# The first group of output weights, loaded as 112 partitions at once and the other 16 two by two

## The chip, the core and the metric

The kernel runs on one core of one Trainium2 chip. The metric is the device time in microseconds (us) of one execution; several executions are timed and their median is given. A profile of one further execution shows what each engine and the DMA queues did in it. TensorE is called PE there, VectorE DVE, ScalarE ACT, GpSimd POOL and SyncE SP.

## The reference

One decode step of attention over a long cache, gated by a small network, with two batch rows, 32 query heads on 8 key heads, 32768 cached keys and a head size of 128, all in float32:

```python
xn = _layernorm(x, axis=-1)                                  # x: 2 x 1 x 512
q = (xn @ wq)                                                # 32 heads of 128
scores = jnp.einsum("bhqd,bhkd->bhqk", q, k) * (Dh ** -0.5)  # k, v: 2 x 8 x 32768 x 128
p = _softmax(scores, axis=-1)
o = jnp.einsum("bhqk,bhkd->bhqd", p, v)
s = o.reshape(B, Sq, Hq * Dh) @ wo                           # wo: 4096 x 512
g = _silu(_B_ref(xn, w1, b1, w2, b2))                        # relu squared network, 512-1792-512
return x + s * g
```

The two caches are 537 MB of the 561 MB that are read. Each value of them is used for the four query heads of its key head and then never again.

## The kernel before, in words

There are 16 sequences (`s`), one for each pair of a key head and a batch row. Keys and values of a sequence come in two halves each, 8 MB a half, 128 partitions of 64 KB. Keys go to `kslots` (three slots of 32 KB a partition, of which a half takes two), values to `vbuf` (64 KB a partition). For a quarter of a sequence's keys `scores` (L240) turns them with DVE transposes (L249) and multiplies them with the query on PE (L254); `softmax` and `probs` make the weights; `values` (L307) multiplies them with the value half (L315).

All the large loads are issued by SP, in the order of the list `loads` (L137 to L142). Each entry names an event and is issued as soon as the event has been given (`give`, L155). The end of the list reads:

```python
    loads += [(("s", NK - 2), load_v, NV - 2), (("v", NV - 3), load_v, NV - 1)]
    loads += [(("s", NK - 1), load_wo, 0), (("s", NK - 1), load_wo, 1), (("v", NV - 2), load_wo, 2), (("v", NV - 2), load_wo, 3)]
```

So the next to last value half goes to `kslots`, the last one to `vbuf`, and behind them come the four groups of output weights, `load_wo(0)` to `load_wo(3)` (L121 to L131). A group is 1024 rows of `wo`, 2 MB, laid out as 128 partitions of 16 KB; two groups share one slot of `kslots`. The first three are one load each (L127), the last is cut along the row into four pieces (`PIECES`, L130). In this document they are called group 0 to group 3, and the last two value halves V30 and V31.

SP takes its instructions in order, and each load carries the waits that the scheduling framework gave it: for what was written or read in its destination before, and one more. The framework gives every load one of eight completion semaphores in turn (they are called semaphore 0 to 7 here); a load that gets a semaphore whose last load SP doesn't know to have landed waits for that load first. In the program as built V30 has semaphore 2, V31 semaphore 3, group 0 semaphore 4, group 1 semaphore 5, group 2 semaphore 6 and the four pieces of group 3 semaphores 7, 0, 1 and 2. The final store on SP (L409) waits for semaphore 4.

At the end `project` (L394) multiplies the attention output with the four groups on PE (L397), group by group and then piece by piece, into one accumulator; two DVE instructions (L406, L407) apply the gate and the residual, and two small stores (L409) write the result.

Of the kernel before, what the change touches and what calls it, by code (L numbers as in the profile page):

```python
# [14 lines left out]
P = 128  # L15
# [15 lines left out]
NT = 4  # L31
HALF = 64 * 128
NEG = -3.0e38
PIECES = ((0, 4), (4, 6), (6, 7), (7, 8))


@with_exitstack
def gqa_decode_kernel(ctx: ExitStack, tc: tile.TileContext, x, kc, vc, wq, wo, w1, b1, w2, b2, out):
    nc = tc.nc
# [12 lines left out]
    NWG = HQ // WG  # L52
# [68 lines left out]
    def load_wo(i):  # L121
        if i % 2 == 0:
            wide[i // 2] = kslots[:, 2 - i].rearrange("p (i j e) -> p i j e", i=2, j=WG)
        t = wide[i // 2][:, i % 2]
        src = wo[i * WG * P:(i + 1) * WG * P, :].rearrange("(p j) e -> p j e", p=P)
        if i < NWG - 1:
            nc.sync.dma_start(t, src)  # L127
        else:
            for j0, j1 in PIECES:
                nc.sync.dma_start(t[:, j0:j1, :], src[:, j0:j1, :])  # L130
        return t  # L131
# [7 lines left out]
    for m in range(2, NV):  # L139
        loads += [(("s", 2 * m - 2), load_k, m), (("v", m - 3) if m > 2 else ("w", 1), load_v, m - 2)]  # L140
    loads += [(("s", NK - 2), load_v, NV - 2), (("v", NV - 3), load_v, NV - 1)]
    loads += [(("s", NK - 1), load_wo, 0), (("s", NK - 1), load_wo, 1), (("v", NV - 2), load_wo, 2), (("v", NV - 2), load_wo, 3)]  # L142
    past = {None}
    done = [0]
# [83 lines left out]
    for t in sc:  # L228
        nc.vector.memset(t, NEG)

# [141 lines left out]
    for n in range(NK):  # L372
        s, i = divmod(n, NT)
# [16 lines left out]

    a_ps = sc[0]
    wot = [take(load_wo, i) for i in range(NWG)]

    def project(i, j0, j1):  # L394
        for j in range(j0, j1):
            for g in range(NG):
                nc.tensor.matmul(a_ps[32 * g:32 * g + 32, :DE], oW[:, i, j, :], wot[i][:, j, g * DE:(g + 1) * DE],  # L397
                                 start=(i == 0 and j == 0), stop=(i == NWG - 1 and j == WG - 1))

    for i in range(NWG - 1):  # L400
        project(i, 0, WG)
    for j0, j1 in PIECES:
        project(NWG - 1, j0, j1)
# [29 lines left out]
```

## Time and profile before

| what | value |
|---|---|
| median of 3 runs | 1311.9 us (1311.33 to 1311.93) |
| the profiled execution | 1312.29 us, of which the span from first to last instruction is 1310.2 us |
| PE busy | 912.5 us, 70% |
| DVE busy | 669.9 us, 51% |
| ACT busy, POOL busy | 130.3 us, 14.9 us |
| read from memory | 561.01 MB, 428 GB/s over the span |
| chain that ended last | DMA 72%, DVE 21%, "issue" 4%, PE 3% |
| mean granted TensorE clock | 0.852 |

Busy time is the sum of what an engine was seen to work. The chain is followed back from the last instruction: at each step to what released it. "Issue" is time in which nothing that the profile shows was waited for. The line of tenths for DMA is the mean over 16 DMA engines, which matters here: it says 9 when all sixteen are busy, and also when one of them is not. The trace holds every single DMA packet with its start, length and size, and for every load the sixteen increments of its completion semaphore, so that the sixteen engines can be told apart: a packet of 64 KB takes about 2.42 us and the next of the same engine starts as it ends.

### The profile page before, as it was taken

To read this page: it belongs to the slowest core of one execution; us is meant where nothing else is said; L and a number is where in the kernel's file an instruction comes from. 1 tells how busy PE (TensorE), PEld (TensorE's weight loads), DVE (VectorE), ACT (ScalarE), POOL (GpSimd) and SP (SyncE) were. 2 spreads that over 40 slices of the span, in tenths; PEclk is the share of its full clock that TensorE was granted. 3 is DMA by queue.
4 is the path that set the end of the run, shared out by engine and by line. 5 is a ranking of instruction groups with operands and counts; after the bars stand their busy time and mean duration, and the time that the engine had idled before them with its cause. 6 is when DMAs were issued, how large, how long until landed. Compare 5 with 4: busy or idle time off the path is not lost.

```text
span 1310.2 us, 11827 instructions
## 1 busy us (share of the span) xinstructions
PE 912.5 (70%) x5054; PEld 230.9 (18%) x5054; DVE 669.9 (51%) x778; ACT 130.3 (10%) x429; POOL 14.9 (1%) x76
## 2 busy tenths in 40 slices
PE   3777675758857677775758767576885767777575
PEld 1221121212202121120212112121220212111023
DVE  2866654446655445665445565444665544566410
ACT  0020010201002020110202001020110202001020
POOL 0000000000000000000000000000000000000000
PEclk9988877888878898887889878778987879888888
DMA  9999999999999999999999999999999999999997
GB/s 404 432 441 435 429 439 426 435 430 433 433 432 433 437 431 433 429 437 429 435 435 427 439 424 439 428 437 437 427 437 428 433 435 431 435 429 431 427 435 307
DMA packets 11042, 561.76 MB, mean 429 GB/s; under 512 B 1239, under 2 KB 1259, under 8 KB 1646
## 3 DMA queue, kind: packets, MB, share of 16 engines
q1 hardware_dynamic: 10952, 561.00, 99.2%
q8 instruction: 39, 0.64, 0.2%
q14 instruction: 13, 0.11, 0.0%
q10 hardware_dynamic: 38, 0.02, 0.0%
HBM read 561.01 MB, written 0.00 MB: 428 GB/s over the span
## 4 chain that ended last, share of the span: by engine, by line
DMA 72%; DVE 21%; issue 4%; PE 3%; ACT 0%; SPq 0%; DVEq 0%
DMA kslots<-in_A_k_cache 66%; DVE kt L249 20%; DMA kslots<-in_A_wo 2%; DMA kslots<-in_A_v_cache 2%; DMA vbuf<-in_A_wq 2%; PE sc L212 1%; PE sc L254 1%; PE o_ps L315 0%; PE y_ps L364 0%; PE h_ps L346 0%; ACT p L275 0%; DVE qr L219 0%; ACT pT L293 0%; PE pT_ps L289 0%; PE sc L397 0%
## 5 line engine op out<-in xcount | busy, mean ns | idle before, releaser
L254 PE MATMUL sc<-kt,qz 128*16 128x512 f32 x2048 | 574.4, 670 | 304.8 <-DVE kt L249 282.9
L249 DVE STREAM_TRANSPOSE kt<-kslots 128x1024 f32<-128x1024 f32 x512 | 583.8, 1206 | 300.5 <-DMA kslots<-in_A_k_cache 300.5
L315 PE MATMUL o_ps<-vbuf,pT 128*16 128x512 f32 x1984 | 232.3, 597 | 10.9 <-DMA vbuf<-in_A_v_cache 10.9
L254 PEld LDWEIGHTS sc<-kt,qz 128*16 128x16 f32 x2048 | 91.4, 98 | 772.8 <-DVE kt L249 619.0
L275 ACT ACTIVATE p<-sc,nm 128x512 f32<-128x512 f32 x64 | 45.7, 740 | 964.9 <-DVE nm L271 964.9
L315 PEld LDWEIGHTS o_ps<-vbuf,pT 128*16 128x16 f32 x1984 | 59.1, 97 | 160.8 <-issue 146.0
L258 DVE TENSOR_REDUCE rm<-sc 128x1 f32<-128x512 f32 x64 | 43.1, 673 | 66.3 <-PE sc L254 66.3
L293 ACT COPY pT<-pT_ps 64x128 f32<-64x128 f32 x256 | 66.4, 259 | 22.6 <-PE pT_ps L289 18.0
L289 PE MATMUL pT_ps<-ident,p 128*128 128x128 f32 x256 | 49.8, 342 | 18.1 <-ACT pT L293 13.8
L327 DVE COPY oT<-oT_ps 128x4 f32<-128x4 f32 x16 | 2.6, 162 | 97.9 <-PE oT_ps L326 97.9
L299 DVE RECIPROCAL r<-l_ps 128x4 f32<-128x4 f32 x16 | 2.9, 182 | 75.5 <-PE l_ps L297 75.5
L289 PEld LDWEIGHTS pT_ps<-ident,p 128*128 128x128 f32 x256 | 36.4, 177 | 28.0 <-ACT pT L293 23.5
L278 DVE TENSOR_REDUCE l<-l 128x1 f32<-128x4 f32 x16 | 2.5, 157 | 49.4 <-ACT p L275 49.4
L235 POOL COPY qz<-qT 32x16 f32<-32x16 f32 x64 | 12.7, 198 | 1078.2 <-PE sc L254 1043.0
L326 PE MATMUL oT_ps<-rs,o_sb 128*128 128x4 f32 x128 | 16.9, 255 | 11.5 <-ACT o_sb L322 11.4
L326 PEld LDWEIGHTS oT_ps<-rs,o_sb 128*128 128x128 f32 x128 | 15.5, 191 | 25.6 <-ACT o_sb L322 25.6
L322 ACT COPY o_sb<-o_ps 128x512 f32<-128x512 f32 x16 | 9.4, 585 | 76.9 <-PE o_ps L315 76.9
L264 PE MATMUL mx_ps<-ident,rm 128*128 128x128 f32 x16 | 5.2, 323 | 14.6 <-DVE rm L262 14.6
L203 PE MATMUL xnT_ps<-ident,xn 128*128 128x128 f32 x4 | 1.1, 431 | 20.1 <-DVE xn L199 20.1
L275 ACT ACTIVATION_READ_ACCUMULATOR p<-sc,nm 128x1 f32 x64 | 12.2, 191 | 0.0
L297 PE MATMUL l_ps<-lh,ones 128*128 128x4 f32 x32 | 8.4, 333 | 3.1 <-ACT pT L293 2.6
L212 PE MATMUL sc<-vbuf,first 128*32 128x512 f32 x64 | 9.4, 751 | 1.6 <-DMA vbuf<-in_A_wq 1.6
(69 smaller groups left out, 119.3 us busy)
## 6 DMA issues: line engine op xcount, KB each, us to landing
kslots<-in_A_k_cache SPq DMA_DIRECT2D x4, 4096.0 KB, 19.4
vbuf<-in_B_w SPq DMA_DIRECT2D x2, 3584.0 KB
kslots<-in_A_wo SPq DMA_DIRECT2D x3, 2048.0 KB
kslots<-in_A_wo SPq DMA_DIRECT2D x1, 1024.0 KB
kslots<-in_A_wo SPq DMA_DIRECT2D x1, 512.0 KB
kslots<-in_A_wo SPq DMA_DIRECT2D x2, 256.0 KB, 31.9
vbuf<-in_A_v_cache SPq DMA_DIRECT2D x31, 30.5
kslots<-in_A_k_cache SPq DMA_DIRECT2D x30
```

What stands on the lines that cost most here:

```text
L212: nc.tensor.matmul(sc[f][32 * g:32 * g + 32, :], xnT[:, d, 0:32], wqt[:, d, cc * 512:(cc + 1) * 512], start=(d == 0), stop=(d == ND - 1))
L235: nc.gpsimd.tensor_copy(qz[s % 2][32 * a:32 * a + 32, :, a * REP:(a + 1) * REP], qT[32 * a:32 * a + 32, b, hkv].rearrange("p h e -> p e h"))
L249: nc.vector.transpose(r.rearrange("p e o w -> p o e w"), kt[:, g * NO:(g + 1) * NO, e0 * 32:(e0 + 2) * 32].rearrange("p o (e w) -> p o e w ...
L254: nc.tensor.matmul(sc[t][32 * g:32 * g + 4 * REP, :], qz[s % 2][:, e0 + e, :], kts[g][:, e].rearrange("p o w -> p (o w)"), start=(e0 + e = ...
L258: nc.vector.tensor_reduce(rm[s][:, t:t + 1], sc[t], axis=AX.X, op=ALU.max)
L275: nc.scalar.activation(p[:, :, t % 2, :, t // 2], sc[t].rearrange("p (o w) -> p o w", w=32), AF.Exp, bias=nm, scale=SCALE, accum_out=l4[:, ...
L289: nc.tensor.transpose(t_ps[:, j * P:(j + 1) * P], p[:, 4 * i + j].rearrange("p c w u -> p (c w u)"), ident)
L293: nc.scalar.copy(sb[64 * a:64 * a + 64, :, c, :, 4 * i:4 * i + 4, :].rearrange("p k g o h -> p o g k h"), v[:, :, :, :4 * REP].rearrange(" ...
L297: nc.tensor.matmul(t_ps[:, :REP], ones, lh, start=True, stop=True)
L315: nc.tensor.matmul(o[32 * g:32 * g + 16, :], pT[s][:, k, c, g, 4 * i:4 * i + 4, :].rearrange("p o h -> p (o h)"), vt[:, lo:lo + 4, :].rear ...
L322: nc.scalar.copy(o_sb, o)
L326: nc.tensor.matmul(t_ps[:, :REP], o_sb[:, i * DH:(i + 1) * DH], r4[:, i, :], start=(i == 0), stop=(i == 3))
```

## The change

Group 0 is loaded by nine instructions in place of one. The first takes partitions 0 to 111, and eight more take two partitions each, 112 and 113, 114 and 115, and so on to 126 and 127. The bytes are the same, and so are the destination, the place in the list and everything else.

```diff
+MAIN = 112
 PIECES = ((0, 4), (4, 6), (6, 7), (7, 8))
...
         t = wide[i // 2][:, i % 2]
         src = wo[i * WG * P:(i + 1) * WG * P, :].rearrange("(p j) e -> p j e", p=P)
-        if i < NWG - 1:
+        if i == 0:
+            nc.sync.dma_start(t[:MAIN], src[:MAIN])
+            for p in range(MAIN, P, 2):
+                nc.sync.dma_start(t[p:p + 2], src[p:p + 2])
+        elif i < NWG - 1:
             nc.sync.dma_start(t, src)
         else:
             for j0, j1 in PIECES:
                 nc.sync.dma_start(t[:, j0:j1, :], src[:, j0:j1, :])
```

The instructions of PE, DVE, ACT and POOL keep their number and order in the program as built. On SP the stretch after V31 reads, with the semaphore that each load uses and the waits that it carries:

```
load of 112 partitions        semaphore 4   waits: DVE
pairs 1 to 5                  5, 6, 7, 0, 1 waits: none
pair 6                        semaphore 2   waits: semaphore 2 (V30)
pair 7                        semaphore 3   waits: semaphore 3 (V31)
pair 8                        semaphore 4   waits: semaphore 4 (the load of 112)
group 1                       semaphore 5   waits: semaphore 5 (pair 1), DVE
group 2                       semaphore 6   waits: semaphore 6 (pair 2), PE
group 3, four pieces          7, 0, 1, 2    waits: the same semaphores (pairs 3 to 6), PE
store                                       waits: semaphore 4 (pair 8), DVE
```

## The prediction

> **What bounds the kernel now.** I began with the page's slices of DMA and the memory rate: all 40 slices but the last are full. Then the chain of waits, read at its end:
>
> ```profile
> 1228.25 0.03 issue
> ...
> 1237.50 29.45 DMA kslots<-in_A_v_cache
> 1266.95 0.04 issue
> 1266.99 5.15 PE o_ps L315 x32
> 1272.15 0.26 SPq L127
> 1272.41 0.04 issue
> 1272.45 0.44 SPq L130
> 1272.89 0.04 issue
> 1272.93 31.77 DMA kslots<-in_A_wo
> 1304.70 0.04 issue
> 1304.74 1.26 PE sc L397 x24
> 1306.01 0.02 issue
> 1306.02 0.47 PE sc L397 x8
> ```
>
> Columns are start, length and what. The kernel ends 0.5 us of PE, two DVE instructions and a store after the last piece of output weights has landed, and that load was issued 31.8 us before: the transfers are what takes time. Next I split the tail into windows (length; busy us and count of PE, PEld, DVE, ACT, POOL; granted clock; DMA share; GB/s):
>
> ```profile
> 1293.00:1297.00 4.00, 3.88 (x50) 1.93 (x42) 0.00 (x0) 0.58 (x1) 0.00 (x0) 1.00 1.03 429
> 1297.00:1299.00 2.00, 2.00 (x55) 1.76 (x58) 0.45 (x2) 0.17 (x1) 0.00 (x0) 1.00 0.95 391
> 1299.00:1301.00 2.00, 1.87 (x71) 1.60 (x60) 0.00 (x0) 0.00 (x0) 0.00 (x0) 1.00 0.63 262
> 1301.00:1303.00 2.00, 1.94 (x64) 1.69 (x64) 0.00 (x0) 0.00 (x0) 0.00 (x0) 1.00 0.55 227
> 1303.00:1305.00 2.00, 1.35 (x45) 1.10 (x47) 0.00 (x0) 0.00 (x0) 0.00 (x0) 1.00 0.45 170
> ```
>
> From 1299 on only some nine of sixteen DMA engines still work. The sixteen increments of V31's semaphore say the same: seven at 1279.55 to 1280.80, nine at 1283.88 to 1286.33. Linking the packets into sixteen chains (a packet starts where the last of its engine ended) shows why: 39 reads of 16 KB, the rows of the "instruction" queue, fall in turn on eight of the chains, five each, about 1 us a time, and a ninth chain lags without them. The late nine set the end; the early seven have 5 to 6.5 us to spare.
>
> Last I read SP's own waits (total us, times, longest), for what an SP instruction waits for besides its data:
>
> ```profile
> SPq L409 <- DMA kslots<-in_A_wo: 16.8, 1, 16.8
> SPq L409 <- DVE fin L407: 15.9, 1, 15.9
> ```
>
> The store needs nothing of the weights' load. It held SP from 1274.4 until group 0 had landed (sixteenth increment at 1291.22) because it shares semaphore 4 with group 0. So such a wait is real in the trace. Today it costs nothing, because nothing is queued behind it.
>
> **The change part by part.**
>
> *One row fewer on each late engine: a gain of 0.61.* Group 0 is 128 rows of 16 KB, eight an engine. A 16 KB packet follows the last after 0.61 us (eight rows: V31's last increment 1286.33, group 0's 1291.22, 4.89 us). With 112 rows each engine has seven: 4.28 us, so that load lands at 1290.61. No load of 112 rows is in the trace; if they spread unevenly, some engine keeps eight and the gain is nothing.
>
> *Sixteen rows on two engines: no cost.* The two-row loads in the trace (x and its four quarters, 2048 and 512 bytes a row) put one row on each of two chains, always the same two, and both of these are free of instruction reads and end among the early seven. I expect the eight pairs there: eight rows more, 4.9 us, against a lead of 5 to 6 us. The price if that cover is gone is a rival below. [...]
>
> *Nine issues in place of one: hidden until V31 lands.* L127's issues take 0.33 to 0.43 us each, some 3 us for eight more, from 1258 on, while the queue holds V30 and V31 (28 us of work). Pair 6 waits for V30, landed at 1266.95: hidden too.
>
> *Pairs 7 and 8: a stop of the queue.* Pair 7 waits for V31 (1286.33), pair 8 for the load of 112 (1290.61). Behind them on SP stand groups 1, 2 and 3, which today are issued by 1274.4. So when the load of 112 ends, no engine but the two of the pairs has a packet left; the early ones have been idle since 1284. Neither DVE nor PE holds group 1 at that point: the keys' slot is free since 1247 and pair 1 landed long before. From the landing at 1290.61:
> - SP wakes, 0.04 (the chain's "issue" pieces); pair 8 is issued: from 0.26 (ACT's two-row load of x, L73) to 0.66 (SP's four-row store, L409). I take 0.4, near SP's other issues (0.33 to 0.49).
> - Group 1's issue to first packet: from 1.02 (first load, issued 0.73, first packet 1.75; the sixteenth engine's at 2.37, so 1.64) to 1.53 (store, 1307.15 to 1308.68). I take 1.3.
> - A first packet from rest: at the start the first packets of 64 KB took 3.10 us to the next, later ones 2.42; 0.69. It could be nothing if the latency does not show for smaller packets.
> - 24 rows and the semaphore writes: from group 0's landing to the last piece's, 1291.22 to 1305.98, 14.76.
> - Packet's end to its increment: 0.47 (1305.53 to 1305.98; 1290.73 to 1291.22). It was inside the landing I start from, and is paid a second time.
> - The two instruction reads of the tail (1295.77 and 1303.05, as PE goes through the projection) took 1.0 and 1.55 us from two of the late chains, which had as much to spare against the last. After the stop all engines restart level, and one such read shows in full: 0 to 1.55, I take 1.0.
>
> Sum: 1290.61 + 0.04 + 0.4 + 1.3 + 0.69 + 14.76 + 0.47 + 1.0 = 1309.27, against 1305.98: **3.3 us later**. Low ends (0.3, 1.02, 0, 0) give 1307.2, +1.2; high ends (0.70, 1.64, 0.69, 1.55) give 1310.4, +4.4. PE's tail behind the last piece (0.47), the two DVE instructions and the store are as before. PE reaches group 0's product at 1295.2 today, after the last value product; pair 8's row lands at about 1293.5, before that, so PE does not become late.
>
> The profiled execution is 1312.29; with 3.3 it is 1315.6. It stands 0.4 above the median of 1311.9, so I predict **1315.2** for the median, 1313.1 to 1316.3 by the terms' own ends. About 0.2% (2.6 us, so 1314.5) is what a measurement of this kernel can tell from no change.
>
> **The rivals.**
>
> *A. The queue does not stop, and the balance is all that is seen* (the other side). If SP's waits end early enough that groups 1 to 3 are queued before the late engines run dry, those lose one row and the two early ones take the rest in their lead: 1305.98 - 0.61, that is **1311.3**. For it: the seven early chains' lead, and that the bytes do not change. Against it: the wait of L409, which lasted to group 0's landing, and pair 8 has the same semaphore. It decides at group 1's issue: before about 1289 (first packet 1.3 later, at the late engines' end) this case holds, after it mine.
>
> *B. The rows get in each other's way.* [...] With seven rows an engine, and with two engines on neighbouring partitions, two may have to share a path. At half speed each a pair takes 1.22; from the early chains' end of V31 (1280.3) with seven rows (4.3) and eight pairs (9.8) the two engines reach 1294.4, and 24 rows (14.7) bring them to 1309.1, still level with the others in my sum. What then counts is the load of 112: each row of a late engine that is shared adds 0.61, and with one to four such rows the time is 1315.8 to 1317.6, **1316.7** in the middle. For it: no row shows such a load, against it: none either. [...]
>
> *C. The pairs fall on late engines.* Then seven and eight rows behind V31 end at 1286.33 + 4.28 + 4.9 = 1295.5, and 24 more at 1310.3: +4.3, **1316.2**, and up to 9 late if they share a path as well (4.9 more). For it: chains that nearly coincide can be exchanged in my linking. Against it: the x loads' chains get no instruction read.
>
> **How the numbers follow.** Mine 0.60, A 0.17, B 0.17, C 0.05, anything else 0.01. Of mine about a fifth lies below 1314.5. So slower is 0.48 + 0.17 + 0.05 = 0.70, the same 0.12 + 0.17 = 0.29, faster 0.01. The range takes my own ends and most of B, 1313.0 to 1317.7; it leaves out A and C's far end.
>
> **What the profile of the changed kernel would show.** SP's waits should list the pairs' line waiting for V31 and then, some 4.3 us, for the load of 112, and group 1 issued at about 1291, not 1258. The tail in windows should show the DMA share near 0.1 for about 2 us around 1291.5, and afterwards close to 1 until nearly the end, since all engines restart level. V31 should land at 1286.3 as before. The load of 112 landing later than 1291 would be B; the last increments of the pieces on two engines alone, well behind the other fourteen, would be C; no gap, A. I would be wrong if the queue holds packets throughout, or if restarting it costs much less than 2.4 us.

## The result and the profile after

The changed kernel takes 1323.7 us (median of 5, 1322.6 to 1324.0) against 1311.9: **11.8 us slower**, ratio 1.0086 (95% interval 1.0075 to 1.0097). The prediction had 1315.2 and a range to 1317.7. The profiled execution took 1322.72, with a span of 1320.9; against the profiled one of before that is 10.4 more, and 10.7 in the span.

The chain of waits of the changed kernel at its end (start, length, what; lines left out are marked):

```profile
1256.73 0.33 SPq L108
1257.06 0.05 issue
1257.11 40.40 DMA kslots<-in_A_wo
1297.52 0.02 issue
1297.53 0.23 SPq L130
...
1299.22 16.20 DMA kslots<-in_A_wo
1315.41 0.04 issue
1315.46 0.64 PE sc L402 x16
```

L130 at 1297.53 is pair 8, held until the load of 112, issued at 1257, has landed. Before, the last weights had been issued by 1274. SP's own waits in the stretch from 1225 on:

```profile
SPq L130 <- DMA vbuf<-in_A_v_cache: 25.2, 1, 25.2
...
SPq L130 <- DMA kslots<-in_A_v_cache: 7.8, 1, 7.8
SPq L130 <- DMA kslots<-in_A_wo: 5.0, 1, 5.0
```

These are pair 7 (V31), pair 6 (V30) and pair 8 (the load of 112), the waits that the prediction named. But the first one is too long. V31 landed at 1292.25, and had landed at 1286.33 before. Windows show why (length; busy us of PE, PEld, DVE, ACT, POOL; granted clock; DMA share; GB/s). Before:

```profile
1280.00:1284.00 4.00, 0.00 (x0) 0.00 (x0) 0.00 (x0) 0.00 (x0) 0.00 (x0) 0.52 1.00 430
1284.00:1288.00 4.00, 1.63 (x8) 0.32 (x12) 0.00 (x0) 0.00 (x0) 0.00 (x0) 0.50 0.93 397
```

After:

```profile
1280.00:1284.00 4.00, 0.00 (x0) 0.00 (x0) 0.00 (x0) 0.00 (x0) 0.00 (x0) 0.50 1.12 250
1284.00:1288.00 4.00, 0.00 (x0) 0.00 (x0) 0.00 (x0) 0.00 (x0) 0.00 (x0) 0.50 0.76 172
...
1296.00:1300.00 4.00, 4.00 (x40) 0.94 (x36) 0.00 (x0) 0.00 (x0) 0.00 (x0) 0.95 0.41 94
...
1304.00:1308.00 4.00, 3.71 (x118) 3.38 (x118) 0.00 (x0) 0.17 (x1) 0.00 (x0) 1.00 1.05 451
```

From 1280 to 1284 all sixteen engines count as busy (share 1.12) and yet move 250 GB/s in place of 430. That is not a stop: a stop is the window at 1296, share 0.41. The single packets say which ones are slow. Start and length of the packets of a late engine (64 KB of V31) and an early one (its last 64 KB, then 16 KB rows of group 0) in the changed kernel:

```
late   1272.96 2.43   1275.38 2.42   1277.80 3.15   1280.93 4.52   1285.44 4.59
early  1275.95 2.42   1278.37 0.70   1279.07 1.31   1280.37 1.13   1281.49 1.13   1282.62 1.25
```

Both fall to about half speed: 64 KB take 4.5 us in place of 2.42, and 16 KB 1.1 to 1.3 in place of the 0.61 of before. It begins at the moment, about 1278, when the first engines go on from V31 to the load of 112 partitions. After the restart, in the window at 1304, all is at full speed again.

### The profile page after: what moved, and what is told of

The parts are those of the page before. It is cut to its first block, busy times and chain, and to the rows that moved or that the text cites. A ratio compares the mean times of both kernels' runs of the same rounds, so it can differ in the third digit from the quotient of the medians.

```text
span 1320.9 us, 11842 instructions
## 1 busy us (share of the span) xinstructions
PE 912.5 (69%) x5054; PEld 232.1 (18%) x5054; DVE 669.9 (51%) x778; ACT 130.2 (10%) x429; POOL 14.9 (1%) x76
## 4 chain that ended last, share of the span: by engine, by line
DMA 71%; DVE 21%; issue 4%; PE 3%; ACT 0%; SPq 0%; DVEq 0%
DMA kslots<-in_A_k_cache 65%; DVE kt L254 20%; DMA kslots<-in_A_wo 4%; DMA vbuf<-in_A_wq 2%; PE sc L217 1%; PE sc L259 1%; PE o_ps L320 1%; PE y_ps L369 0%; PE h_ps L351 0%; ACT p L280 0%; DVE qr L224 0%; ACT pT L298 0%; PE pT_ps L294 0%; DVE rm L263 0%; PE sc L402 0%
## 5 line engine op out<-in xcount | busy, mean ns | idle before, releaser
L280 ACT ACTIVATION_READ_ACCUMULATOR p<-sc,nm 128x1 f32 x64 | 12.2, 190 | 0.0
L402 PE MATMUL sc<-kslots,oW 128*32 128x128 f32 x256 | 9.8, 302 | 3.2 <-issue 2.9
L320 PE MATMUL o_ps<-kslots,pT 128*16 128x512 f32 x64 | 9.9, 785 | 2.1 <-DMA kslots<-in_A_v_cache 2.1
```

Of the source, the lines that this page charges most:

```text
L280: nc.scalar.activation(p[:, :, t % 2, :, t // 2], sc[t].rearrange("p (o w) -> p o w", w=32), AF.Exp, bias=nm, scale=SCALE, accum_out=l4[:, ...
L320: nc.tensor.matmul(o[32 * g:32 * g + 16, :], pT[s][:, k, c, g, 4 * i:4 * i + 4, :].rearrange("p o h -> p (o h)"), vt[:, lo:lo + 4, :].rear ...
```

## The experiments

Theory **shared path**: the load of 112 partitions makes engines write partitions which other engines are writing, and whoever shares a path goes at half speed. No trace tells which engine writes which partition, and none shows a path: both are the author's assumption, and what the runs can show is when the rates fall, and by how much. Rivals: **stop** (SP's waits are all of it), **pairs** (the eight small loads slow the others), and for the runs in the middle **tail only**, **uneven rows** and **source**. All times are medians beside runs of the kernel before on the same chip: 1312.06 for the stop, the load of 112 alone, 112 and 16, and the eight extra pairs; 1312.15 for the four fours and for the value half split by columns and by partitions; 1312.23 for the four extra pairs and the other source.

### The stop alone

```diff
-            nc.sync.dma_start(t, src)
+            nc.sync.dma_start(t[:, 0:7], src[:, 0:7])
+            for p in range(0, P, 16):
+                nc.sync.dma_start(t[p:p + 16, 7:8], src[p:p + 16, 7:8])
```

> Group 0 in nine loads again, so that SP's waits and the stop of the queue stay, but the first takes all 128 partitions (seven eighths of each row) and the eight others 16 partitions of 2 KB each, one row an engine; no load of 112 partitions and no pairs of 16 KB rows. Theory 'shared path' (the 112-partition load makes engines write where others write, and both halve): V31 lands at 1286.3 as before, not at 1292; the first of the nine lands 4.3 us later, group 1 is issued at about 1291.1, and the time is that of the stop alone, 3 to 4 us over before, about 1315.5. Theory 'stop' (the wait for V31 and for the first load is all of the loss, and V31's late landing follows from it): all of the loss stays, about 1323.

Measured: 1316.85, ratio 1.0036 (1.0023 to 1.0049), 4.8 over. V31 landed at 1286.43, the first of the nine at 1290.81, group 1 was issued at 1291.24. Two windows of it:

```profile
1280.00:1284.00 4.00, 0.00 (x0) 0.00 (x0) 0.00 (x0) 0.00 (x0) 0.00 (x0) 0.60 0.99 413
...
1288.00:1292.00 4.00, 4.00 (x28) 0.90 (x24) 0.00 (x0) 0.00 (x0) 0.00 (x0) 0.62 0.28 101
```

The rate does not halve at 1280, and there is a gap at 1288 to 1292. The stop is real and costs 4.8 (4.0 between the profiled executions), above the 3 to 4 expected, and it does not make V31 late.

### The load of 112 alone

```diff
-            nc.sync.dma_start(t, src)
+            nc.sync.dma_start(t[:112], src[:112])
```

> Group 0 as the load of 112 partitions alone; the 16 last partitions are not loaded, which leaves that part of the product out. No pair, and no wait that stops the queue. Theory 'shared path': V31 still lands 5 to 6 us late, at about 1292, and the end is later than before by some 5 us although 256 KB less are read; about 1317. Theory 'stop': nothing is left of the loss, V31 at 1286.3 and 0.6 us less than before, 1311.3. Theory 'pairs' (the eight two-partition loads slow the others): the same as 'stop', 1311.3.

Measured: 1321.56, ratio 1.0075 (1.0060 to 1.0090), 9.5 over, with 256 KB less to read. V31 landed at 1292.51.

```profile
1280.00:1284.00 4.00, 0.00 (x0) 0.00 (x0) 0.00 (x0) 0.00 (x0) 0.00 (x0) 0.50 1.12 250
1284.00:1288.00 4.00, 0.00 (x0) 0.00 (x0) 0.00 (x0) 0.00 (x0) 0.00 (x0) 0.50 0.86 176
```

The same halving with no pair and no wait behind it: "stop" and "pairs" both fall as the main cause. The size, 9.5, is above the 5 that "shared path" expected. Here groups 1 and 2 follow at once, and the likely reading is that they collide with the late engines' rows of the load of 112 as well. That load landed 8.2 us after V31; in the changed kernel, where the stop keeps the others away, 5.3 after.

### 112 and 16, and 112 and four fours

```diff
+            nc.sync.dma_start(t[:112], src[:112])
+            nc.sync.dma_start(t[112:], src[112:])
```

> Group 0 as 112 partitions in one load and the other 16 in one more, one row an engine; the queue is not stopped. Theory 'shared path': V31 late by 5 to 6 us as in the changed kernel, and the sixteen rows slow one another too; 6 to 8 us over before, about 1319. Theory 'stop': no loss, 1311.9 within 0.5. Theory 'pairs': no loss either, since no engine gets more than eight rows.

Measured: 1323.59, ratio 1.0090 (1.0074 to 1.0107), 11.5 over, V31 at 1292.05; "shared path" had expected 6 to 8. The second form takes partitions 112 to 127 in four loads of four. Groups 1 and 2 are then issued by 1273, so that the queue does not stop:

```diff
+            nc.sync.dma_start(t[:112], src[:112])
+            for p in range(112, P, 4):
+                nc.sync.dma_start(t[p:p + 4], src[p:p + 4])
```

> The change with four loads of four partitions in place of eight of two: 112 partitions first as there, but five loads, so that groups 1 and 2 and the first piece of group 3 are issued before the queue can run empty. Theory 'shared path alone': the stop costs nothing beside the collisions, and the time is 10 to 12 us over before, about 1323, as in the changed kernel. Theory 'sum' (the collisions and the stop of 4.8 us add up): about 7 over, 1319.

Measured: 1324.35, ratio 1.0094 (1.0079 to 1.0109), 12.2 over. So the loss of the changed kernel is there in full without the stop. The two costs do not add up: 9.5 and 4.8 stand beside 11.8. A reason that fits is that nothing new collides while the queue stands still: the load of 112 landed 5.3 us after V31 in the changed kernel, and 9.2 after it in the form with fours.

### Extra pairs

```diff
             nc.sync.dma_start(t, src)
+            for p in range(112, P, 2):
+                nc.sync.dma_start(kslots[p:p + 2, 1, 0:4096].rearrange("p (j e) -> p j e", j=WG), src[p:p + 2])
```

> Group 0 whole in one load of 128 partitions, and the eight pairs behind it as extra loads of the same rows into a slot that nobody reads any more (256 KB more are read); SP's waits and the stop are as in the changed kernel. Theory 'shared path': V31 lands at 1286.3, since no load of 112 is there; the stop costs its 3 to 4 us plus one more row on every engine (0.6) and some more where the pairs meet group 0's last rows, 4 to 6 us over before, about 1317. Theory 'pairs': V31 at 1292 and 11 to 12 us over before, about 1323.

Measured: 1320.42, ratio 1.0066 (1.0051 to 1.0081), 8.4 over, with V31 at 1285.84. The time can't be used: in the order of the program the slot was still to be read, for V30, so that `values` of V30 waited for the pairs (until 1294) and took part of its values from what they had written. What can be used is V31's landing: it is on time with eight pairs in the queue and no load of 112. That is weak evidence against "pairs", since only one row of the first pair had landed by then (1285.51); the load of 112 alone decides.

A cleaner form puts four pairs behind group 2, after `values` of V30. Its expectation says that no wait stops the queue, which is not so for the four pieces of group 3:

```diff
+        if i == 2:
+            nc.sync.dma_start(t, src)
+            for p in range(112, 120, 2):
+                nc.sync.dma_start(kslots[p:p + 2, 1, 0:4096].rearrange("p (j e) -> p j e", j=WG), src[p:p + 2])
```

> All of before, with four pairs (partitions 112 to 119, 16 KB rows) as extra loads behind group 2, into a slot that is no longer read; 128 KB more, two engines get four rows more, no wait stops the queue. Theory 'shared path': the pairs' engines have the time (4 rows at 0.6 to 1.2 against 5 us of lead), but the rows go to partitions that two late engines write, each of which loses up to four rows' time: 0.5 to 2.5 us over before. Theory 'lead' (the step of the prediction: the two engines have the time, so nothing is lost): within 0.4 of before.

Measured: 1314.0 (median of 11), ratio 1.0014 (1.0005 to 1.0023), 1.8 over for 128 KB more; the profiled execution, 1314.70, is the slowest of the eleven. SP's waits, and one window beside the same one of before:

```profile
SPq L134 <- DMA kslots<-in_A_wo: 16.4, 3, 7.3
```

Before:

```profile
1296.00:1300.00 4.00, 3.88 (x97) 3.59 (x100) 0.45 (x2) 0.29 (x2) 0.00 (x0) 1.00 0.91 374
```

With four pairs:

```profile
1296.00:1300.00 4.00, 4.00 (x104) 3.76 (x108) 0.45 (x2) 0.17 (x1) 0.00 (x0) 1.00 0.86 245
```

The four loads in front take four semaphores, so each piece waits for an earlier load, and the last one was issued at 1304.08, when group 2 had landed. That is not where the time went. Group 2 itself landed at 1304.07, 3.1 later than before (1301.01), and from there to the last increment it is 4.9 us, against 5.0 before. The loss lies in front, while the pairs' rows were written: the rate fell to 245 GB/s, and each row of 16 KB that began between 1296 and 1300 took 0.68 to 1.93 us, where before 0.61 was the rule. So the two engines had the time, and it was lost on the others. "Shared path" forecast that, for two late engines; but none of the packets of that stretch, of any size, was as short as before. Why so many slow down is open.

### One value half in the middle of the run

To see the loss without the tail, value half 10 alone was split in `load_v`, in four ways. By columns:

```diff
+        if m == 10:
+            nc.sync.dma_start(t[:, :14336], src[:, :14336])
+            nc.sync.dma_start(t[:, 14336:], src[:, 14336:])
```

> A control in the middle of the run: value half 10 (8 MB) in two loads of 128 partitions, the first seven eighths of each row and the last eighth. All theories: no cost, within 0.5 us of before.

By partitions, as in the change:

```diff
+            nc.sync.dma_start(t[:112], src[:112])
+            nc.sync.dma_start(t[112:], src[112:])
```

> Value half 10 as 112 partitions in one load and 16 in another; nothing at the tail is changed and no wait stops the queue. Theory 'shared path' (engines that write one another's partitions halve): the load of 112 goes on at half the rate, 7 rows of 64 KB at 4.5 us instead of 2.42, so 15 us more, and the loads beside it lose too; 10 to 20 us over before. Theory 'tail only' (the loss needs the end of the run, where the queue runs empty): no cost, since 30 more loads lie behind it.

By partitions, in halves:

```diff
+            nc.sync.dma_start(t[:64], src[:64])
+            nc.sync.dma_start(t[64:], src[64:])
```

> Value half 10 as partitions 0 to 63 in one load and 64 to 127 in another: four rows an engine, a power of two. [...] Theory 'uneven rows' (seven rows an engine, a count that does not divide, is what costs): no cost, within 0.5.

Not split, but read from elsewhere:

```diff
+            nc.sync.dma_start(t.rearrange("p (a f) -> p a f", a=2),
+                              rows(vc, s)[u * CHUNK:(u + 1) * CHUNK].rearrange("(a p r) d -> p a (r d)", a=2, p=P))
```

> Value half 10 again, into all 128 partitions with one load, but each partition's row is read from two places 4 MB apart (two runs of 32 KB) in place of one; the keys' order in that half is changed with it, so that its part of the output is another. It moves the source and leaves the destination. Theory 'shared path' on the destination's side: no cost, within 0.5. Theory 'source' (what costs in the loads of 112 and 64 rows is where they read): a cost of several us.

| value half 10 in | time | over | ratio, 95% interval |
|---|---|---|---|
| two loads of 128 partitions, cut by columns | 1312.01 | -0.1 | 1.0001 (0.9992 to 1.0010) |
| partitions 0 to 111, and 112 to 127 | 1340.09 | 27.9 | 1.0214 (1.0199 to 1.0230) |
| partitions 0 to 63, and 64 to 127 | 1336.77 | 24.6 | 1.0185 (1.0168 to 1.0202) |
| one load, rows read from two places | 1311.79 | -0.4 | 0.9998 (0.9989 to 1.0007) |

Windows of the kernel with 112 and 16:

```profile
470.00:480.00 10.00, 8.26 (x72) 2.49 (x71) 2.00 (x8) 3.53 (x9) 0.80 (x4) 1.00 1.02 441
...
490.00:500.00 10.00, 6.17 (x20) 1.15 (x20) 7.56 (x7) 0.00 (x0) 0.00 (x0) 0.58 1.01 223
...
520.00:530.00 10.00, 0.00 (x0) 0.00 (x0) 0.00 (x0) 0.00 (x0) 0.00 (x0) 0.50 1.07 138
```

And with 64 and 64:

```profile
490.00:500.00 10.00, 2.46 (x5) 0.39 (x6) 3.85 (x4) 0.00 (x0) 0.00 (x0) 0.50 1.00 204
...
520.00:530.00 10.00, 0.00 (x0) 0.00 (x0) 0.00 (x0) 0.00 (x0) 0.00 (x0) 0.52 0.99 210
```

Every engine is busy all the time (with 64 and 64 a share of 0.99 to 1.03) at half the rate (204 to 211 GB/s from 490 to 530, where before had 421 to 446), for 45 to 50 us, and at 520 to 530 PE and DVE run dry. With 112 and 16 the rate falls further, to 138, when the sixteen last partitions come: packets of 64 KB then take 7.2 to 8.9 us. "Tail only" falls (the list has 47 loads behind it, not the 30 of the expectation, and they hide nothing, since the run is bound by transfers throughout: before, DMA is 90% busy or more in 39 of the profile's 40 slices), "uneven rows" falls (64 and 64 goes at half speed as well, 204 to 211 GB/s), and "source" has nothing for it (moving the source alone costs nothing, -0.4). The 10 to 20 expected of 112 and 16 was too little. With 64 and 64 the half takes 40 us in place of 19.4, from the landing of the load in front of it on the first engine to its own there. And with 112 and 16 that load in front, half of a sequence's keys, lands at 492.4 in place of 488.3: the neighbours lose too.

That splitting the destination's partitions costs (24.6 and 27.9), and moving the source alone does not (-0.4), is what the runs show. By what means the loads slow one another was not shown, nor why the four extra pairs slowed so many engines.

## Why the prediction was wrong, point by point

*What bounds the kernel, and the tail's late engines:* right. *SP's waits and their order:* right; pair 8 waited for the load of 112, group 1 was issued 0.34 us after its landing (0.44 in the sum). *The stop's price:* the sum had 3.3, of which 0.6 was a gain of the shorter load; alone it measured 4.8 (3.0 to 6.4), and there the first load is shorter too (4.38 behind V31, where the whole group took 4.89). So it was sized a little low, within the interval: from group 1's issue to the end it took 18.85 in the changed kernel and 19.0 alone, where the sum had 18.2; the steps up to the issue took 0.34 and 0.43, where it had 0.44.

*V31 lands at 1286.3 as before:* **this is the step that failed.** The sum took V31's landing over unchanged and gave no reason; group 0 does stand behind V31 in the queue. But the engines go on one by one: five of the early seven began group 0 at 1278.4 to 1279.5, while the late nine had two or three packets of V31 to go, and from then on both loads went at half speed. V31 landed 5.9 later. The late engines had some 6 us of V31 left, and half speed for that is an estimate of 6 more.

*The load of 112 takes 4.28 on a late engine:* 5.27 measured, 1.0 more. Seven rows an engine, an estimate before, is what the packets show (an early engine writes seven from 1278.37 to 1286.30, a late one seven from 1290.03 to 1295.87), but a row took 0.62 to 1.31 in place of 0.61. With these the sum closes, from profile to profile: 3.3 (predicted) + 5.9 (V31) + 1.0 (load of 112) - 0.1 (issue) + 0.6 (restart to the end) = 10.7, and the last increments are 1305.98 and 1316.71. The medians differ by 11.8; the profiled executions lie 0.4 above the one and 1.0 below the other.

*Sixteen rows on two engines cost nothing:* wrong in its reason. The two engines had the lead, but four extra pairs beside the old loads cost 1.8, for rows that slowed down on the other engines. That an engine has time to spare does not mean that its rows cost the others nothing. What the eight pairs cost in the changed kernel itself was not separated.

*The rivals.* B came nearest, with rows that slow one another, at a third of the size at most: it priced rows within the load of 112 only, 0.6 to 2.4, and the slowing took 6.9 (5.9 and 1.0). No run shows its term, half speed for two engines that share a path (1.22 us a pair, and C's 4.9 more); what the runs showed in its place is the time of the packets, 4.3 to 5.1 us for 64 KB in place of 2.42 and 1.0 to 1.3 for 16 KB in place of 0.61 between 1279.5 and 1290. B left out what that load does to the load before it, though its half speed, as an estimate for as long as the two loads overlap, would have bounded that: at the tail, the 5 to 6 us between the early and the late engines. Its own sign, the load of 112 landing later than 1291, did show. A and C did not happen: the queue did stop, and the last two increments came 0.4 us behind the other fourteen for group 1 and 0.5 for the last piece, not far behind.

## What to carry to other kernels

In these runs one load with another number of partitions slowed the load in flight beside it as much as itself: at the tail, 64 KB of V31 took 4.3 to 5.1 us in place of 2.42, and the rows of 16 KB between 1279.5 and 1290 took 1.0 to 1.3 in place of 0.61. Cut a large load along the free dimension and keep all 128 partitions: here the cut by partitions lost 9.5 to 12.2 us at the tail without any stop of the queue and 24.6 to 27.9 in the middle of the run, and the cut by columns, in the middle, nothing. And read the number of GB/s beside the busy share: in these runs a share of 1.0 at half the rate (0.99 at 210 GB/s, from 520 to 530 with 64 and 64) went with loads that slowed one another, and a low share (0.28 at 101 GB/s, from 1288 to 1292 in the stop alone) with a queue that had nothing to do.

## What the runs showed of the hardware that was not expected

- The DMA engines drift apart: the sixteen increments of one load lie 0.5 us apart at the start of the run and 6.8 for V31. Over the run 39 reads of instructions, 16 KB each, take 1.0 to 1.1 us apiece from eight engines in turn; a ninth lags without them, and why is open. So before the change group 0's first packet began at 1279.24, 6.6 us ahead of the end of V31's last one (1285.83).
- Seven engines that write the load of 112 slow all nine that still write V31, from 2.42 us for 64 KB to between 4.3 and 5.1 from 1279.5 on, and within two packets; none of them got away at full speed.
- The loss of one split load in the middle of the run, 24.6 to 27.9 us, is above the 19.4 more that its own 8 MB take at half the rate (an estimate: eight packets an engine at 2.42). With 112 and 16 the keys' load in front of it landed 4.1 us late, so the loads beside it pay too.
- Four extra loads of two partitions, 128 KB in all, slowed all rows while they were written, from 0.61 us for 16 KB to between 0.68 and 1.93, and cost 1.8 us.
